# First batch of a fused attention and feed-forward kernel: another order of its prologue, without bank marking

## The chip, the cores and the metric

The kernel runs on one core of a Trainium2 chip. The metric is the device time of one execution in microseconds (us); lower is better. The kernel before takes 943.23 us (median of 3 runs, 943.13 to 943.5). A difference of more than 2% would count as faster or slower. Every profile lists the mean clock that was granted to TensorE; where it matters it is given.

## The reference

Eight batches of eight heads: queries of 576 tokens attend to keys and values that are first averaged over 8 tokens (72 pooled tokens). The result, 4608 rows of 512, goes through a hidden layer of 2048 with a periodic activation and an output layer.

```python
k_p = k.reshape(B, H, Sp, 8, D).mean(axis=3)          # v_p likewise
scores = scale * np.matmul(q, k_p.transpose(0, 1, 3, 2))
attn = softmax(scores)                                # sum + 1e-9
x = np.matmul(attn, v_p)                              # -> [4608, 512]
h = x @ w_in
g = h + sin(alpha * h) ** 2 / (alpha + 1e-9)
out = g @ w_out
```

All is in 32-bit floats. The kernel makes the two matrix products by Strassen's scheme (seven products of half size instead of eight), which is why sums of parts of w_in and of parts of x occur below.

## The kernel before

The time is that of a long, dense sequence of TensorE products. Ahead of it stands a prologue, `first_batch`: attention of batch 0, four score tiles of 128 rows (a fifth of 64 rows follows in the first products). One tile goes like this: TensorE makes scores, VectorE their maxima, ScalarE the exponentials, VectorE sums and reciprocals, GpSimd multiplies, TensorE transposes the probabilities, ScalarE and VectorE copy the transposes, TensorE multiplies with the values.

```python
def score_exp(i):
    sums = self.sm.tile([P, H], F32, name="sm")
    ps, odd = products(i)                               # scores, TensorE
    ...                                                 # max, shift: VectorE
    for hp in range(NP):                                # even heads; sums on the way
        nc.scalar.activation(out=E(n, i, h, h + 1), in_=ps[:n, hp:hp + 1, :], func=AF.Exp,
                             bias=mx[:n, hp:hp + 1], accum_out=sums[:n, h:h + 1])
    nc.scalar.activation(out=ex[:n, i, 1::2, 0:Sp], in_=..., func=AF.Exp)   # odd heads
    def rest(eng=nc.vector):
        ...                                             # sums of the odd heads, + 1e-9
        divide(i, sums, eng)
    return rest

def first_batch(self):
    ...                                                 # loads, transposed keys
    A.q_t(0)
    A.q_t(1)
    norm, v = {}, self.sum_v_rows(0)
    for i in range(4):
        norm[i] = A.score_exp(i)
        if i < 3:
            A.q_t(i + 2)
        if i:
            next(v)                                     # pooled values, TensorE
        if i:
            norm[i - 1](nc.gpsimd)
        if i > 1:
            self.mark(i - 2)
            A.a_t(i - 2, 0)                             # transposes of the probabilities
            A.a_t(i - 2, 1)
    ...                                                 # loads of the next keys, queries, w_in
    norm[3]()
    self.mark(2)
    A.a_t(2, 0)
    A.a_t(2, 1)
    self.mark(3)
    self.mark(4)
    A.a_t(3, 0)
    A.a_t(3, 1)
    for hp in range(4):
        A.values(hp)
    self.combine_w_in(0, 0)                             # sums of w_in, VectorE
    self.sums_of_x(0, 0)
    self.sums_of_x(0, 1)
```

The marking is four idle products with the identity, which write a PSUM bank whole. It is there because later a ScalarE copy fills a bank and TensorE accumulates onto the copy:

```python
def mark(self, i):
    ps = self.bank([P, 4, P], i)
    for j in range(4):
        self.nc.tensor.matmul(ps[:, j, :], self.ident[:], self.ident[:], start=(j == 0), ...)

def left0(G=G, Q=before):
    G.b6 = bank()
    nc.scalar.copy(out=G.b6[:], in_=G.b1[:])            # products 6 and 3 accumulate onto it
```

The hidden layer then runs in groups of seven products, in the order 1, 5, 6, 2, 7, 3, 4 (the numbers are those of the scheme, so product 7 is the fifth in time), and work of other kinds is hung into numbered slots, one for each product, before it:

```python
at(0, self.combine_w_in, 0, 1)
at(1, lambda: self.rest.append(A0.score_exp(4)))        # fifth tile
at(2, lambda: self.rest.pop()())
...
for J in range(1, 4):                                   # w_in parts 1 to 3
    at((4, 10, 14)[J - 1], self.combine_w_in, J, 0)
    at((6, 12, 20)[J - 1], self.combine_w_in, J, 1)
```

## Time and profile before

| | |
|---|---|
| time | 943.23 us (3 runs, 943.13 to 943.5) |
| span of the profiled run | 941.8 us |
| TensorE | 98% busy |
| first query transposes | 13.19 us |
| first values product | 33.95 us |
| product 7 of the first group | 46.84 us |

The busy line and the chain are shown in the prediction. This is the list of what TensorE waited for: the instruction that waited, what released it, then us in total, the number of times, and the longest.

```profile
PE ps_at L269 <- DVE aT L271: 1.2, 1, 1.2
PE bank L497 <- ACT bank L535: 0.8, 2, 0.6
PE bank L497 <- DVE as L373: 0.8, 1, 0.8
```

Apart from waits for the first loads these are all the waits of weight: 2.8 us. Idle time is thus no large prize; the other prize is TensorE work that computes nothing, the marks.

### The profile page before, as it was taken

How to read it: one execution, taken by the hardware profiler on the slowest of the kernel's cores; microseconds unless marked ns; L12 is line 12 of the kernel's file. 1: busy time of each engine (PE TensorE's matmuls, PEld its weight loads, DVE VectorE, ACT ScalarE, POOL GpSimd, SP SyncE). 2: the span in 40 equal slices, each digit the busy share in tenths (PEclk: the TensorE clock that was granted, in tenths of full speed). 3: DMA queues.
4: the chain of work that ended last, by engine and by line, in shares of the span. 5: the costliest groups of instructions: out<-in, count | busy, mean ns of one | idle time of the engine just before them, and what ended most of it. 6: DMA issues, size and time to landing. Idle time of an engine off the chain costs nothing.

```text
span 941.8 us, 17546 instructions
## 1 busy us (share of the span) xinstructions
PE 920.8 (98%) x6859; PEld 819.5 (87%) x6859; DVE 694.5 (74%) x1043; ACT 445.6 (47%) x1042; POOL 197.9 (21%) x214
## 2 busy tenths in 40 slices
PE   5999999999999999999999999999999999999997
PEld 3687787887878878787888899999999999999997
DVE  5779584766748677484346889988989798889794
ACT  5477576585857758677696651212111111211111
POOL 1628354453634536250000000000000000000000
PEclk9999999999999999999999999999999999999999
DMA  9645457666576663745624545353435444343501
GB/s 230 178 142 173 122 190 167 201 160 201 154 195 194 167 191 101 186 148 146 224 90 143 187 141 150 103 164 89 148 105 135 118 127 127 117 135 93 160 13 38
DMA packets 139777, 137.82 MB, mean 146 GB/s; under 512 B 49024, under 2 KB 108176, under 8 KB 139696
## 3 DMA queue, kind: packets, MB, share of 16 engines
q1 hardware_dynamic: 138624, 135.53, 49.8%
q10 hardware_dynamic: 1072, 1.19, 0.5%
q8 instruction: 54, 0.88, 0.4%
q14 instruction: 27, 0.22, 0.1%
HBM read 74.46 MB, written 47.19 MB: 129 GB/s over the span
## 4 chain that ended last, share of the span: by engine, by line
PE 94%; DVE 2%; ACT 2%; DMA 1%; issue 0%; SPq 0%; ACTq 0%; DVEq 0%
PE bank L497 45%; PE bank L778 29%; PE ps_y L778 12%; PE ps_o L311 3%; PE ps_sc L210 2%; DMA q<-in_q_dram 1%; DVE as L373 1%; PE ps_qt L191 1%; PE ps_at L269 1%; ACT s L503 1%; PE bank L460 1%; DVE home L470 0%; PE ps_or L320 0%; PE bank L122 0%; DVE a L373 0%
## 5 line engine op out<-in xcount | busy, mean ns | idle before, releaser
L497 PE MATMUL bank<-home,a 128*128 128x256 f32 x1152 | 267.1, 383 | 0.8 <-ACT bank L535 0.8
L497 PEld LDWEIGHTS bank<-home,a 128*128 128x128 f32 x1152 | 214.8, 190 | 35.8 <-ACT bank L535 2.7
L497 PE MATMUL bank<-home,as 128*128 128x256 f32 x864 | 202.4, 383 | 1.2 <-DVE as L373 0.8
L497 PEld LDWEIGHTS bank<-home,as 128*128 128x128 f32 x864 | 161.2, 190 | 26.4 <-ACT bank L523 3.2
L107 POOL TENSOR_TENSOR kvin<-kvin 72x512 f32<-72x512 f32 x112 | 122.2, 1091 | 164.2 <-DMA kvin<-in_v_dram 108.8
L778 PE MATMUL bank<-s,wb 128*128 128x144 f32 x896 | 119.4, 286 | 0.4 <-ACT bank L891 0.4
L778 PEld LDWEIGHTS bank<-s,wb 128*128 128x128 f32 x896 | 113.7, 190 | 0.7 <-ACT bank L891 0.6
L510 ACT ACTIVATE s<-s,c 128x256 f32<-128x256 f32 (+1 forms) x216 | 110.0, 573 | 0.0
L503 ACT ACTIVATE s<-h,al 128x256 f32<-128x256 f32 x144 | 65.2, 501 | 79.6 <-DVE h L476 79.6
L476 DVE TENSOR_TENSOR h<-bank,p 128x512 f32<-128x512 f32 x72 | 49.2, 683 | 62.8 <-ACT s L510 28.2
L891 ACT COPY bank<-bank 128x144 f32<-128x144 f32 x56 | 14.7, 263 | 145.7 <-PE bank L778 144.3
L503 ACT ACTIVATE s<-bank,al 128x256 f32<-128x256 f32 x144 | 59.9, 467 | 33.5 <-PE bank L497 10.5
L564 DVE TENSOR_TENSOR h<-bank,s 128x512 f32<-128x512 f32 x36 | 24.6, 684 | 49.7 <-ACT s L510 49.0
L910 ACT COPY bank<-bank 128x144 f32<-128x144 f32 x56 | 14.7, 263 | 88.2 <-PE bank L778 88.2
L252 POOL TENSOR_TENSOR ex<-ex,sm 128x576 f32<-128x576 f32 (+1 forms) x38 | 42.7, 1148 | 60.0 <-DVE sm L251 29.1
L733 DVE TENSOR_TENSOR s<-r 128x576 f32<-128x576 f32 x64 | 48.1, 752 | 0.8
L564 DVE TENSOR_TENSOR h<-h,s 128x1024 f32<-128x1024 f32 x36 | 46.2, 1283 | 0.0
L733 DVE TENSOR_TENSOR s<-x 128x576 f32<-128x576 f32 x48 | 36.2, 753 | 7.6 <-PE ps_y L778 6.7
L868 ACT COPY bank<-ps_y 128x288 f32<-128x288 f32 x56 | 21.4, 383 | 38.7 <-PE ps_y L778 38.7
L147 DVE STREAM_TRANSPOSE tr<-q 128x1024 f32<-128x1024 f32 (+1 forms) x24 | 18.1, 808 | 26.8 <-DMA g_bridge<-h 21.3
L778 PE MATMUL bank<-s,a 128*128 128x144 f32 x256 | 36.6, 286 | 0.0
L778 PE MATMUL ps_y<-s,a 128*128 128x144 f32 x256 | 36.6, 286 | 0.0
(142 smaller groups left out, 1436.4 us busy)
## 6 DMA issues: line engine op xcount, KB each, us to landing
g_bridge<-h SPq DMA_DIRECT2D x72, 512.0 KB
r<-g_bridge SPq DMA_DIRECT2D x31, 1152.0 KB
out_dram<-o SPq DMA_DIRECT2D x128, 72.0 KB
q<-in_q_dram SPq DMA_DIRECT2D x8, 1024.0 KB
kvin<-in_k_dram SPq DMA_DIRECT2D x28, 288.0 KB
kvin<-in_v_dram SPq DMA_DIRECT2D x28, 288.0 KB
a<-in_moe_w_in_dram SPq DMA_DIRECT2D x16, 256.0 KB
q<-tr SPq DMA_DIRECT2D x48, 80.0 KB
```

The source lines that it names most:

```text
L107: (eng or nc.gpsimd).tensor_tensor(out=o, in0=t[:, :, 0:w], in1=t[:, :, w:2 * w], op=OP.add)
L210: nc.tensor.matmul(ps[e][r:r + q.shape[-1], hp, :], q[s], kb[s, hp, :], start=True, stop=True)
L252: eng.tensor_tensor(out=E(n, i, 0, H), in0=E(n, i, 0, H), in1=sm[:n].unsqueeze(2).to_broadcast([n, H, Sp]), op=OP.mult)
L311: nc.tensor.matmul(ps[64 * e:64 * e + 64, :], vp[:, h, :], x, start=True, stop=True)
L476: add = lambda o, x, y: nc.vector.tensor_tensor(out=o, in0=x, in1=y, op=OP.add)
L497: nc.tensor.matmul(ps[:, jj, :], self.A[p][:, kk, f * P:(f + 1) * P], x[:, kk, :], start=(start and jj == 0 and kk == 0), stop=(kk == 1), ...
L503: nc.scalar.activation(out=G.s[:, i, jj, j, :], in_=src[:, jj], func=AF.Sin, scale=self.al[:, f:f + 1])
L510: nc.scalar.activation(out=x, in_=x, func=AF.Square, scale=self.c[:, f:f + 1])
L564: add = lambda o, x, y: self.nc.vector.tensor_tensor(out=o, in0=x, in1=y, op=OP.add)
L733: tt = lambda o, x, y, op: nc.vector.tensor_tensor(out=o, in0=x, in1=y, op=op)
L778: nc.tensor.matmul(out, W[:, J // 2, J % 2, :], A[:, J, :], start=(start and J == 0), stop=(J == self.NJ - 1), skip_group_check=True)
L868: nc.scalar.copy(out=x0[:], in_=yz[:, 0:1, :].to_broadcast([P, 2, T]))
```

## The change

It wants TensorE to reach the hidden layer earlier. The scores are issued one tile ahead, so that no engine waits for the next one's turn; the softmax sums come out of one reduction over all heads; the marks go, because the first two values products now write the two banks that need it (2 and 4) whole; the sums of w_in's first part are made while TensorE multiplies with the values. Also the fifth tile's division moves from VectorE to GpSimd and three w_in sums from slot 20 to slot 15.

```diff
-        def score_exp(i):
+        def soft(i, ps):
-            sums = self.sm.tile([P, H], F32, name="sm")
-            ps, odd = products(i)
+            even, odd = ps
 ...
-                nc.scalar.activation(out=E(n, i, h, h + 1), in_=ps[:n, hp:hp + 1, :], func=AF.Exp,
-                                     bias=mx[:n, hp:hp + 1], accum_out=sums[:n, h:h + 1])
+                nc.scalar.activation(out=E(n, i, h, h + 1), in_=even[:n, hp:hp + 1, :], func=AF.Exp, bias=mx[:n, hp:hp + 1])
 ...                                     (rest() goes; norm(i) was there already)
         def values(hp):
-            ps = self.ps_a.tile([P, 4 * P], F32, name="ps_o", tag="a")
+            ps = self.bank([P, 4 * P], 2 + 2 * hp) if b == 0 and hp < 2 else self.ps_a.tile([P, 4 * P], F32, name="ps_o", tag="a")
 ...                                     (mark() goes)
-        norm, v = {}, self.sum_v_rows(0)
+        v = self.sum_v_rows(0)
+        ps = A.products(0)
+        A.q_t(2)
         for i in range(4):
-            norm[i] = A.score_exp(i)
+            A.soft(i, ps)
             if i < 3:
-                A.q_t(i + 2)
-            if i:
+                ps = A.products(i + 1)
+                if i < 2:
+                    A.q_t(i + 3)
                 next(v)
             if i:
-                norm[i - 1](nc.gpsimd)
-            if i > 1:
-                self.mark(i - 2)
-                A.a_t(i - 2, 0)
-                A.a_t(i - 2, 1)
+                A.norm(i - 1)
+        A.a_t(0, 0)
+        A.a_t(0, 1)
+        A.norm(3)
+        A.a_t(1, 0)
+        A.a_t(1, 1)
 ...                                     (loads as before)
-        norm[3]()
-        self.mark(2)
-        A.a_t(2, 0)
-        A.a_t(2, 1)
-        self.mark(3)
-        self.mark(4)
-        A.a_t(3, 0)
-        A.a_t(3, 1)
+        for i in (2, 3):
+            A.a_t(i, 0)
+            A.a_t(i, 1)
+        self.combine_w_in(0, 0)
+        self.combine_w_in(0, 1)
         for hp in range(4):
             A.values(hp)
-        self.combine_w_in(0, 0)
 ...
-            at(0, self.combine_w_in, 0, 1)
-            at(1, lambda: self.rest.append(A0.score_exp(4)))
-            at(2, lambda: self.rest.pop()())
+            at(1, lambda: A0.soft(4, A0.products(4)))
+            at(2, A0.norm, 4)
 ...
-                at((6, 12, 20)[J - 1], self.combine_w_in, J, 1)
+                at((6, 12, 15)[J - 1], self.combine_w_in, J, 1)
```

More of the change, by code (lines that the diff above doesn't have):

```diff
@@ L227, in exp @@
             nc.scalar.activation(out=e, in_=e, func=AF.Exp, scale=scale)
-        def score_exp(i):
+        def soft(i, ps):
             n = rows[i]
-            sums = self.sm.tile([P, H], F32, name="sm")
-            ps, odd = products(i)
+            even, odd = ps
             mx = self.sm.tile([P, NP], F32, name="mx")
-            nc.vector.tensor_reduce(out=mx[:n], in_=ps[:n], axis=AX, op=OP.max, negate=True)
+            nc.vector.tensor_reduce(out=mx[:n], in_=even[:n], axis=AX, op=OP.max, negate=True)
             shift(i, 1, odd)
@@ L238, in score_exp @@
                 h = 2 * hp
-                nc.scalar.activation(out=E(n, i, h, h + 1), in_=ps[:n, hp:hp + 1, :], func=AF.Exp,
-                                     bias=mx[:n, hp:hp + 1], accum_out=sums[:n, h:h + 1])
+                nc.scalar.activation(out=E(n, i, h, h + 1), in_=even[:n, hp:hp + 1, :], func=AF.Exp, bias=mx[:n, hp:hp + 1])
             nc.scalar.activation(out=ex[:n, i, 1::2, 0:Sp], in_=ex[:n, i, 1::2, 0:Sp], func=AF.Exp)
-            def rest(eng=nc.vector):
-                nc.vector.tensor_reduce(out=sums[:n, 1::2], in_=ex[:n, i, 1::2, 0:Sp], axis=AX, op=OP.add)
-                nc.vector.tensor_scalar(out=sums[:n], in0=sums[:n], scalar1=1e-9, scalar2=None, op0=OP.add)
-                divide(i, sums, eng)
-            return rest
         def divide(i, sm, eng):
@@ L321, in values_rest @@
             to_x(ps[:], slice(0, NP), 512, 64)
-        return SimpleNamespace(**{f.__name__: f for f in (k_t, q_t, score, exp, score_exp, norm, new_a, a_t, turn, move, values, values_rest)})
+        return SimpleNamespace(**{f.__name__: f for f in (k_t, q_t, products, soft, score, exp, norm, new_a, a_t, turn, move, values, values_rest)})
     def load_alpha(self, rows):
@@ L454, in bank @@
         return self.ps_m.tile(shape, F32, name=f"bank{i}")
-    def mark(self, i):
-        ps = self.bank([P, 4, P], i)
-        for j in range(4):
-            self.nc.tensor.matmul(ps[:, j, :], self.ident[:], self.ident[:], start=(j == 0), stop=(j == 3), skip_group_check=True)
     def sums_of_x(self, u, n):
@@ L948, in run @@
                 self.qm, self.qt, self.kp, self.vp = {}, {}, {}, {}
-                self.bt, self.left, self.group, self.rest, self.turn = {}, [], None, [], 0
+                self.bt, self.left, self.group, self.turn = {}, [], None, 0
                 self.R = {}
```

## The prediction

> **What bounds the kernel now.** I read the page's busy table first, then the chain that ended last, then that chain in order of time over the first 100 us, then the timeline of each engine there.
>
> ```profile
> PE 920.8 (98%) x6859; PEld 819.5 (87%) x6859; DVE 694.5 (74%) x1043; ACT 445.6 (47%) x1042; POOL 197.9 (21%) x214
> PE 94%; DVE 2%; ACT 2%; DMA 1%; issue 0%; SPq 0%; ACTq 0%; DVEq 0%
> ```
>
> TensorE is busy for 98% of the span and carries 94% of the chain, so what counts is how early it gets through the prologue. After 100 us the waits of its matmuls add up to 0.4 us (one, in the output phase). So whatever the first 100 us gain reaches the end unchanged, and nothing later can add to it. The change touches only these first 100 us. The chain there (start, us, what):
>
> ```profile
> 23.76 1.09 PE bank L460 x8
> 24.85 0.87 PE ps_at L269 x8
> ...
> 27.33 1.09 PE bank L460 x8
> 28.42 0.87 PE ps_at L269 x8
> 29.29 0.89 PE bank L460 x8
> 30.19 0.87 PE ps_at L269 x8
> 31.06 1.79 PE bank L460 x16
> 32.85 0.45 PE ps_at L269 x4
> ...
> 33.95 3.68 PE ps_o L311 x16
> ...
> 38.28 0.86 DVE home L470 x2
> ...
> 44.67 1.30 ACT ex L239 x8
> ...
> 46.30 0.49 ACT bank L535
> ...
> 46.84 1.99 PE bank L497 x8
> ```
>
> L460 is the bank marking: five marks of four 128x128 products, 1.09 + 1.09 + 0.89 + 1.79 = 4.86 us, all on the chain. Up to 33.3 us TensorE runs without a break; L269 are the transposes of the probabilities, L311 the values products. From 38.3 to 46.8 us the chain leaves TensorE: VectorE makes the sums of x (L470) and of w_in (L373), then the maximum of the fifth score tile (L235), ScalarE its exponentials (L239, L241) and the bank copy L535 for which the product at 46.84 waits. In that stretch TensorE sits idle 0.79 us (until 42.89, for L373) and 0.3 us (until 46.84). Later idle times: 0.21 us until 76.34, 0.59 us until 80.65 (both ACT copies) and 1.20 us until 90.92, where a transpose waits for VectorE's copy L271, which stood behind three w_in sums.
>
> VectorE in that stretch (start, us, instruction):
>
> ```profile
> 34.37 0.68 DVE L373 TENSOR_TENSOR as<-a,a 128x512 f32<-128x512 f32 x1
> ...
> 39.86 1.75 DVE L470 TENSOR_TENSOR home<-home,home 128x512 f32<-128x512 f32 x1
> 41.54 1.21 DVE L373 TENSOR_TENSOR as<-as,a 128x512 f32<-128x512 f32 x1
> 42.67 0.94 DVE L373 TENSOR_TENSOR a<-a,a 128x512 f32<-128x512 f32 x1
> ```
>
> The same operation takes 0.68 us alone and 0.94, 1.21 or 1.75 us while GpSimd makes its key sums (29.8 to 43.05 us).
>
> **What the Trainium skill says.** "PSUM — Partial Sum Buffer", section "The four PSUM rules": only TensorE sets the bits that make a later product accumulate; a ScalarE copy into a bank leaves them as they are. Here banks filled by a ScalarE copy (L523, L535) are accumulated onto, so they must first have been written whole by TensorE. Only the first two such banks (numbers 2 and 4) see no whole product before; values products of 128x512 into exactly those do a mark's work for nothing. The trace shows no such bits. "SBUF — State Buffer", section "Who interferes with whom": a VectorE operation with two SBUF inputs and a GpSimd operation reading SBUF lock each other out; the four durations above agree, and reductions do not contend (0.44 to 0.46 us throughout). "ScalarE: Activation LUTs", section "What ACT_TABLE_LOAD costs": a load takes about 1283 ns (trace: 1.28 us at 15.80), and activations in a row overlap by about 93 ns. "TensorE: Matmul & The Clock Gate", section "Part 1: The HAM clock gate": after an idle window of about 3.4 us the array falls to half clock. The trace shows a warm-up: the 64x72 products take 0.38 us at 15.19 and 0.22 us from 18.04 on.
>
> **The change, part by part.** I replay the new order of each engine (taken from the built program) with the durations of this trace.
>
> *Scores ahead, one table load later.* Products 0 to 3, the query transposes and the value sums keep their durations; with neither mark 0 nor the first transposes in between, products 3 start at 23.7 instead of 25.72 us and the last value sum (L125, 0.95) ends at 25.3 instead of 27.3 us. ScalarE now copies the third query tile before the exponentials: the copy waits for the transposes (17.45), and the table load follows it, 18.0 to 19.25 instead of 15.80 to 17.08. The first exponentials are 2.2 us later, but TensorE's next need, the copy of query tile 3, is met by 21.06, well before 23.7.
>
> *Sums in one operation.* The exponentials lose their accumulator reads (four a tile; starts 0.30 us apart become, as an estimate from duration minus the page's overlap, 0.22): about 0.3 us per tile off ScalarE. VectorE replaces a reduction of 0.44, an addition of 0.17 and its wait by one reduction over eight heads of 0.76 (row L259): about 0.1 us more per tile. Neither binds.
>
> *Marks gone, but a wait in their place.* After 25.3 us the chain is that of the last tile. ScalarE: copy of the value sums at 25.3, exponentials of tile 3 from 25.8 to 27.1 (ends with L241's form). VectorE: sum and reciprocal 27.2 to 28.2. GpSimd multiplies 28.3 to 29.45 (1.15). TensorE transposes tile 3 at 29.5 to 30.4 (0.87), ScalarE copies 29.97 to 30.55, and the values products start at 30.6 instead of 33.95. TensorE idles about 1.0 us (a transpose waits for a buffer that ScalarE frees at 27.6) plus 0.5 us and 0.2 us. Check: 4.86 removed less some 1.5 of new idle time is 3.35 us, the difference 33.95 - 30.6.
>
> *w_in sums during values.* Values end at 34.3 instead of 37.6. VectorE starts its eight two-input sums at 31.0 instead of in two pieces until 44.2. Besides GpSimd, starts are 0.86, 1.13 or 1.68 us apart, so eight take about 8.9 us and end at 39.9. The first sum of x is ready at 36.2, the second at 37.9, the third at 39.05. TensorE: product 1 34.3 to 36.2, fifth scores to 36.85, then three products of 1.77 each, to 42.2, without a wait. The fifth tile's maximum is at 39.9, its exponentials 40.4 to 41.6, the bank copy to 42.15: just in time for the product at 42.2 instead of 46.84. That gains 9.2 - 7.9 = 1.25 us more. Sum: 3.35 + 1.25 = **4.6 us**.
>
> *Fifth tile's division on GpSimd.* It queues behind the key sums, ends at some 43.6 to 44.0; its transposes are due at 44.0. No loss, barely.
>
> *Three w_in sums moved earlier (slot 20 to 15).* They leave the place where they cost 1.20 us (90.92) and stand before four softmax sums and the addition h (L476, in before at 83.51) which the seventh group's last product must await, as it writes the same bank. I find that addition ending 1.2 us after the product could start. So the 1.2 us change place: net 0, give or take 0.7.
>
> **Rivals.**
> 1. *A transfer holds the lead back.* In the issue queue's waits, w_in's second part lands at 42.9 to 45.1 us and queries 1 at 41.4 to 42.3. They are issued behind the fourth key load, which waits for GpSimd's first key sum; that moves only some 0.4 us. TensorE wants the queries at 44.6 and the weights at 50.7, VectorE its first of them at 43.9: against this rival, by 1 us. If it held, it would take back up to 2 us: 940.5.
> 2. *VectorE becomes the bound.* Its eight sums beside GpSimd end just in time. If each costs 0.3 us more, the fifth softmax comes 2 us later and the gain falls to 2.5: 940.7. For it: durations up to 1.75 us. Against it: GpSimd is through at 42.2 anyway.
> 3. *The array's clock falls.* Between 26.2 and 30.5 us TensorE works only some 2.7 of 4.4 us. If that lowered the clock, values and the first products would take longer by 2 to 4 us: 940.5 to 943. No gap is longer than 1.1 us, so I give it one in twelve.
> 4. *Both stalls of the moved sums vanish,* if GpSimd's value sums end earlier: 1.2 us more gain, 937.4.
>
> **Range and chances.** 943.23 - 4.6 = 938.6. Rivals 1 to 3 pull up to 941.2, the fourth and a shorter softmax chain down to 937.0. Over 2% would need 18.9 us; all marks and all the idle times listed above make 4.86 + 3.1 = 8 us, so faster is next to excluded; slower would need a lasting clock loss.
>
> **What would show it.** Right: no L460 rows; values products from about 30.6; product seven of the first group near 42.2; the idle time at 90.9 gone and one of about 1.2 us some 5 us earlier for an addition of h; busy time of TensorE down by some 4.5 us. Wrong: values later than 32 us, matmuls of 128x256 slower than 0.38 us after the gap, or TensorE waiting for a DMA between 42 and 60 us.

## The result, and the profile after

The changed kernel takes 940.89 us (median of 4 runs, 939.70 to 941.32); the kernel before took 943.37 us on the same chip (4 runs, 943.13 to 944.28). The ratio is 0.997, 95% interval 0.9953 to 0.9987. That is the same within 2%, as predicted, and inside the predicted range, but the gain is 2.5 us by the medians and not 4.6. A ratio here and below is the mean time of one kernel's fast runs over that of the other's fast runs in the same rounds, so it is not quite the ratio of the medians quoted.

The busy line and the chain's shares of the changed kernel:

```profile
PE 916.1 (98%) x6819; PEld 814.8 (87%) x6819; DVE 691.3 (74%) x1036; ACT 444.3 (47%) x1022; POOL 200.1 (21%) x216
PE 93%; DVE 3%; DMA 2%; ACT 1%; issue 1%; SPq 1%; POOL 0%; DVEq 0%; ACTq 0%; POOLq 0%
```

TensorE works 4.7 us less, as the marks are gone. But VectorE has a larger share of the chain than before, and a transfer has come onto it. The chain's pieces in order of time (start, us, what):

```profile
27.36 1.16 POOL ex L244
...
29.87 1.94 PE bank L304 x8
...
36.90 8.23 DMA a<-in_moe_w_in_dram
...
45.22 0.06 DVE as L366
...
46.51 0.34 DVE aT L263
...
46.98 0.63 PE ps_qt L191 x4
```

L304 is the values product: it starts at 29.87 us and not at 33.95. From 36.9 us the chain runs through a load of the second part of w_in, VectorE's first sum of it (L366), and a copy (L263) that stands behind that sum in VectorE's queue, to a query transpose. That is a new path. What TensorE waited for now (columns as before):

```profile
PE bank L484 <- DVE h L463: 1.5, 1, 1.5
PE ps_at L261 <- ACT aT L263: 0.9, 1, 0.9
PE bank L484 <- ACT bank L522: 0.8, 2, 0.6
PE ps_qt L191 <- DVE aT L263: 0.4, 1, 0.4
...
PE ps_at L261 <- DVE aT L263: 0.3, 1, 0.3
PE ps_at L261 <- POOL ex L244: 0.3, 1, 0.3
```

The wait of 1.2 us for a copy of transposes has shrunk to 0.3; the wait for w_in sums is gone; 0.9 and 0.4 us are new, and so is 1.5 us for the addition of h. The two that matter most on TensorE's timeline (start, us, operation, count, in brackets the idle time before and what ended it):

```profile
41.66 1.99 PE L484 MATMUL bank<-home,a 128*128 128x256 f32 x8 [0.19 <-ACT bank L522]
81.07 1.99 PE L484 MATMUL bank<-home,a 128*128 128x256 f32 x8 [1.50 <-DVE h L463]
```

The first is product 7 of the first group, 46.84 us in the kernel before; the second is the last product (product 4) of the third group. VectorE's timeline in the same kernel:

```profile
30.28 0.68 DVE L366 TENSOR_TENSOR as<-a,a 128x512 f32<-128x512 f32 x1
...
32.88 1.75 DVE L366 TENSOR_TENSOR as<-a,as 128x512 f32<-128x512 f32 x1
...
45.22 0.69 DVE L366 TENSOR_TENSOR as<-a,a 128x512 f32<-128x512 f32 x1 [3.00 <-DMA a<-in_moe_w_in_dram]
```

The w_in sums begin at 30.28, beside the values products, and the fifth tile follows them early enough. At 45.22 VectorE has stood still for 3.00 us for the load.

Two profiles do not start alike: the queries land at a different moment in each. So stretches are compared, from the first query transpose ("query start") on. The last column is the sum: from there to the second product (product 5) of the fourth group, behind which the two kernels do the same.

| profile | query start | to first values product | to product 7 of group 1 | to product 1 of group 2 | to product 5 of group 4 | sum |
|---|---|---|---|---|---|---|
| before | 13.19 | 20.76 | 12.89 | 8.43 | 36.62 | 78.70 |
| before, second profile | 13.37 | 20.50 | 12.88 | 8.44 | 36.45 | 78.27 |
| changed | 12.55 | 17.32 | 11.79 | 8.97 | 37.15 | 75.23 |
| changed, second profile | 12.99 | 17.81 | 11.80 | 8.92 | 36.89 | 75.42 |

Means: 20.63 to 17.57 (gain 3.1), 12.89 to 11.80 (gain 1.1), 8.44 to 8.95 (loss 0.5), 36.5 to 37.0 (loss 0.5): 3.2 us in all.

### The profile page after: what moved, and what is told of

Same layout as the page of the kernel before. It is cut to its first block, busy times and chain, and to the rows that moved or that the text cites. A ratio compares the mean times of both kernels' runs of the same rounds, so it can differ in the third digit from the quotient of the medians.

```text
span 937.9 us, 17446 instructions
## 1 busy us (share of the span) xinstructions
PE 916.1 (98%) x6819; PEld 814.8 (87%) x6819; DVE 691.3 (74%) x1036; ACT 444.3 (47%) x1022; POOL 200.1 (21%) x216
## 4 chain that ended last, share of the span: by engine, by line
PE 93%; DVE 3%; DMA 2%; ACT 1%; issue 1%; SPq 1%; POOL 0%; DVEq 0%; ACTq 0%; POOLq 0%
PE bank L484 44%; PE bank L764 29%; PE ps_y L764 12%; PE ps_o L304 3%; PE ps_sc L210 2%; DMA q<-in_q_dram 1%; DMA a<-in_moe_w_in_dram 1%; PE ps_qt L191 1%; PE ps_at L261 0%; DVE sm L251 0%; DVE h L463 0%; PE ps_or L313 0%; PE bank L122 0%; DVE as L366 0%; DVE a L366 0%
## 5 line engine op out<-in xcount | busy, mean ns | idle before, releaser
L244 POOL TENSOR_TENSOR ex<-ex,sm 128x576 f32<-128x576 f32 (+1 forms) x40 | 45.0, 1149 | 55.5 <-DVE sm L243 30.7
L764 PE MATMUL ps_y<-r,wb 128*128 128x144 f32 x256 | 36.6, 286 | 0.0
L764 PE MATMUL bank<-r,wb 128*128 128x144 f32 x256 | 36.6, 286 | 0.0
```

Of the source, the lines that this page charges most:

```text
L244: eng.tensor_tensor(out=E(n, i, 0, H), in0=E(n, i, 0, H), in1=sm[:n].unsqueeze(2).to_broadcast([n, H, Sp]), op=OP.mult)
L764: nc.tensor.matmul(out, W[:, J // 2, J % 2, :], A[:, J, :], start=(start and J == 0), stop=(J == self.NJ - 1), skip_group_check=True)
```

## The experiments

All outputs are right. Edits are given against the changed kernel unless something else is said.

**Controls.** The unedited changed kernel once more, and at the end the unedited kernel before for a second profile.

> The changed kernel unedited, beside the others. Theory A (the prologue gains 3.4 us at the values products and 4.5 us at the seventh product, as predicted, and some is given back later to w_in's second part landing at about 45 us and to the moved sums): 940.9 us, give or take 0.6; in the profile the values products stand 17.8 us after the first query copy starts (29.87 - 12.07; before: 33.95 - 12.71 = 21.24), and VectorE idles 2 to 3.5 us until its first w_in sum of the second group, near 45. Theory B (the gap between 3.9 us in the profiles and 2.5 us in the medians is only the moment at which the first queries land): the distance from the query copy to product one of the second group is the same 38.6 us in every profile, and only the copy's start (12.0 to 13 us) moves.

939.77 us (5 runs, 939.63 to 941.16) against 943.80 (11 runs, 942.73 to 945.09); ratio 0.996, interval 0.9947 to 0.9972. With the first result this puts the gain at 2.8 to 3.8 us, and the sum of stretches gives 3.2. Theory A had the wait for the load right (2.96 us) but its time, 940.9 give or take 0.6, lay above the 939.77 measured. Theory B's fixed distance of 38.6 us failed: it is 39.0 here (51.52 less 12.51).

> The kernel before, unedited, for a second profile of it: if the array's warm-up moment is as random there as in the changed kernel, its first fast 64x72 product comes 4 to 8.3 us after the first query transpose, and the stretch from there to the first values product lies between 20.5 and 21.5 us; product seven of the first group stands 12.8 to 13.0 us after the first values product, as in its first profile (12.89). A value of 11.8 there would show that the later w_in sums cost it nothing in some runs.

One run of 943.52 us, of unknown state. Product seven stands 12.88 us after the first values product and the stretch to values is 20.50: the profile of before was no accident.

**Marks alone: the kernel before without its marks,** its first two values products in banks 2 and 4. Edit against the kernel before:

```diff
-            ps = self.ps_a.tile([P, 4 * P], F32, name="ps_o", tag="a")
+            ps = self.bank([P, 4 * P], 2 + 2 * hp) if b == 0 and hp < 2 else self.ps_a.tile([P, 4 * P], F32, name="ps_o", tag="a")
 ...
-                self.mark(i - 2)
-        self.mark(2)
-        self.mark(3)
-        self.mark(4)
```

> The kernel before with one part of the change alone: no bank marking, and the first two values products write banks 2 and 4. Worked out from the trace of before: the values products start at 31.3 instead of 33.95 us and everything behind follows, so 2.6 us off before, as much as the whole change brings in the medians. Rival (the marks filled time in which TensorE would have waited for the last tile's softmax anyway): under 1 us off before.

945.93 us (6 runs, 942.47 to 946.43), ratio 1.0016, interval 1.0004 to 1.0029: slower than the kernel before. The expectation missed. Five runs had a granted clock of 0.991 or 0.992 and took 945.67 to 946.43; the sixth had 0.998 and took 942.47. TensorE's timeline of the profiled run, which was one of the five:

```profile
29.01 1.07 PE L269 MATMUL ps_at<-ident,ex 128*72 128x128 f32 x8 [1.56 <-POOL ex L252]
30.94 1.65 PE L269 MATMUL ps_at<-ident,ex 128*72 128x128 f32 x8 [0.86 <-DVE ex L252]
32.52 3.68 PE L311 MATMUL bank<-aT,vp 72*64 72x512 f32 x8
...
39.54 3.78 PE L497 MATMUL bank<-home,a 128*128 128x256 f32 x8
```

The eight values products take 3.68 us (1.94 in the changed kernel), the eight products of the hidden layer 3.78 (1.99). The same run by stretches; the second column is the length, then busy us and instructions of TensorE, its weight loads, VectorE, ScalarE and GpSimd, then the granted clock and the transfers:

```profile
28.00:32.00 4.00, 2.13 (x15) 1.78 (x16) 3.29 (x6) 1.50 (x4) 3.84 (x5) 0.90 0.00 0
32.00:44.00 12.00, 12.00 (x39) 5.11 (x39) 5.73 (x9) 3.31 (x6) 8.00 (x9) 0.50 0.97 283
```

TensorE was busy for only 2.13 of 4.00 us, and the clock went to 0.50. By the packed trace's own record (trace.npz) it stayed there from 31.22 to 44.87 us, although TensorE then worked without a break. In the changed kernel TensorE is busy for 3.44 us of the same four, and the granted clock is 1.00 throughout. So in the old order the marks did something besides marking: they filled the gaps. To test that reading, two marks went back into the gaps, one ahead of the transposes of tile 2 and one ahead of those of tile 3 (against the kernel just told):

```diff
+        self.mark(0)
         A.a_t(2, 0)
         A.a_t(2, 1)
+        self.mark(1)
         A.a_t(3, 0)
```

> The kernel of e4_marks_only (before without marks), with two marks of four products put back, not where TensorE has work, but into its two waits for the softmax (1.56 us before the third tile's transposes, 0.86 us before the fourth's). Clock theory: in e4 the clock fell to half from 31 to 44.6 us because TensorE idled; filled with work that nobody needs, the waits keep it at full speed, the mean clock is 0.998 to 0.999 in all runs, and the kernel is 1.3 to 2 us faster than before (e4's one run without the fall was 1.3 us faster). Rival (the clock fell for another reason, or by chance): runs of about 946 us at a clock of 0.991 or 0.992 as in e4.

942.19 us (5 runs, 940.96 to 943.19), before 944.18 there (9 runs, 942.65 to 945.72), ratio 0.9979, interval 0.9965 to 0.9994; clock 0.998 to 1.0 in all five runs. More idle products and a shorter time, with the clock kept in all five runs: the fall of the clock was what had made the marks-only kernel slow. TensorE's longest wait in that stretch is now 0.67 us. Removing the marks from the old order is thus worth 1.3 us (the one run at 0.998) to 2 us (with two marks kept) if the clock holds, and costs some 2 if it does not.

**The marks in the new order.** The changed kernel with all five marks back ahead of the transposes:

```diff
+        self.mark(0)
         A.a_t(0, 0)
 ...
+        self.mark(1)
         A.a_t(1, 0)
 ...
         for i in (2, 3):
+            self.mark(i)
+            if i == 3:
+                self.mark(4)
             A.a_t(i, 0)
```

> The changed kernel with the five marks put back in front of the transposes, everything else as changed. Theory: the marks fill part of about 1.5 us in which TensorE waits for the last tile's softmax, so 4.46 us of marks (five of 0.89) cost 3 to 3.5 us, and the kernel stands 0.5 to 1.5 us below before. Rival (the reordering is the gain, the marks are nearly free beside the waits): within 1.5 us of the changed kernel.

942.73 us (5 runs, 942.11 to 944.06), ratio 0.9986, interval 0.9973 to 0.9998. Values start 20.11 us after query start, against 17.32 and 17.81: the marks cost 2.3 to 2.8 us there, some 2.4 us by the ratios (0.9986 less 0.996 of 943 us), less than the 3 to 3.5 expected. The new order and the earlier w_in sums alone give some 1.3 us.

**The w_in sums in their old place.**

```diff
-        self.combine_w_in(0, 0)
-        self.combine_w_in(0, 1)
         for hp in range(4):
             A.values(hp)
+        self.combine_w_in(0, 0)
 ...
+            at(0, self.combine_w_in, 0, 1)
```

> The changed kernel with the first group's w_in sums where they stood before: one behind the values products, three in the first slot of the hidden stage. Prediction's step: 1.25 us of gain come from these sums during the values, so the product seven of the first group starts about 12.9 us after the values products instead of 11.8, and the kernel is 1.1 us slower than the changed one. Rival (what is gained there is lost again to w_in's second part, which lands at 44 to 46 us whatever is before it): less than 0.5 us slower.

942.33 us (5 runs, 942.24 to 944.19), ratio 0.9983, interval 0.997 to 0.9996. The stretch from values to product seven is 13.55 us instead of 11.80, and TensorE's timeline has the old wait back:

```profile
41.68 1.97 PE L484 MATMUL bank<-home,as 128*128 128x256 f32 x8 [0.79 <-DVE as L366]
```

This part alone is worth 1.75 us by the profile, more than the 1.25 predicted. The earlier the values come, the more a late sum seems to cost: with the sums in their old place the stretch is 12.89 us where values start 20.76 us after query start (before), 13.26 at 19.34 (two marks in the gaps) and 13.55 at 18.26 (here).

**The transfer.** The second part of w_in loaded right behind the first, so that nothing can wait for it:

```diff
         self.load_w_in_part(0)
+        self.load_w_in_part(1)
 ...
         self.load_q(1)
-        self.load_w_in_part(1)
```

> The second part of w_in is asked for right after the first, before the keys of batch 1, in the time from 24 to 33 us in which no transfer runs. Theory A: the 3.0 us for which VectorE stands idle until 45.22 shrink below 0.7 us, the 0.44 us wait of a query transpose at 46.98 goes, and the kernel is 0.4 to 1.5 us faster than the control, with less spread between its runs. Rival (the wait is hidden: TensorE had work until then): within 0.3 us of the control.

940.12 us (5 runs, 939.57 to 941.15), ratio 0.9962, interval 0.995 to 0.9974: no difference from the control on the same chip (0.996), so the gain of 0.4 to 1.5 us that theory A expected did not come. VectorE's sum starts without a wait at 43.26:

```profile
43.26 0.71 DVE L366 TENSOR_TENSOR as<-a,a 128x512 f32<-128x512 f32 x1
```

The 0.4 us of TensorE's wait went, and a wait of 0.26 us for GpSimd's division of the fifth tile (at 45.03) came in its place; the stretch shrank from 8.92 to 8.67. Other profiles show that the load's landing is a matter of chance: in the next experiment, which does not touch it, VectorE waited for it only 0.56 us instead of 3.00 and 2.96, and the stretch was 8.36, no longer than in the kernel before:

```profile
44.10 1.27 DVE L366 TENSOR_TENSOR as<-a,a 128x512 f32<-128x512 f32 x1 [0.56 <-DMA a<-in_moe_w_in_dram]
```

So the transfer takes 0.5 us in some executions and nothing in others. That lies within the scatter of the times.

**The three moved sums back in slot 20.**

```diff
-                at((6, 12, 15)[J - 1], self.combine_w_in, J, 1)
+                at((6, 12, 20)[J - 1], self.combine_w_in, J, 1)
```

> The three w_in sums of the last group back from slot 15 to slot 20. Prediction's step: net 0, give or take 0.7 us, against the control: the 1.50 us wait of the product behind the addition h at 81.07 goes, and a wait of about 1.2 us of a transpose behind VectorE's copy returns near 86. Rival: the move costs more than it brings, and this run is faster than the control by 0.8 us or more. Other rival: the move is the gain it was meant to be, and this run is slower by 1.2 us.

940.44 us (5 runs, 940.13 to 940.85), ratio 0.9963, interval 0.9951 to 0.9975: neutral. The wait of 1.20 us at a transpose is back (at 87.09) and the one of 1.5 us is gone, as the swap in the prediction has it.

**The fourth tile's division first.** `A.norm(3)` ahead of `A.a_t(0, 0)` instead of behind it, so that VectorE's copies do not stand before the chain of the last tile:

> The changed kernel with the last tile's sum and reciprocal put in front of the first copies of transposes on VectorE. If the chain of the last tile (sum, reciprocal, GpSimd's division, transposes, copy) sets the start of the values products, as predicted, they start 0.5 us earlier: 17.3 us instead of 17.8 us after the first query transposes of the profile, and the kernel is 0.3 to 0.6 us faster. Rival (the transposes' wait of 0.88 us for ScalarE's copies sets it): no difference.

940.57 us (5 runs, 940.24 to 941.11), ratio 0.9961, interval 0.9949 to 0.9974: nothing to see in the time, and the half us expected did not come. Its profile has 17.97 us to the first values product, against 18.33 in the profile of the preceding experiment; but that difference is not the edit's.

That last remark needs explaining. In every profile but that of the last experiment below, the 64x72 products of the scores are slow at first (0.32 to 0.38 us) and fast later (0.22 us). The moment at which the array becomes fast is kept in the packed trace: its record of the granted clock has its first entry there, and the clock columns print 1.00 for the time before it. In the changed kernel that is at 16.23 us (four query transposes take 0.89 us at 15.72 and 0.66 us at 17.28). Counted from query start it came after 3.57 to 6.18 us in the twelve profiles without idle products ahead of the queries. In the new order without marks the stretch to values follows it: 17.32 us at a delay of 3.68, 17.55 at 4.21, 17.64 at 4.65, 17.81 at 5.01, 18.26 at 6.02, 18.33 at 6.18. The run with the division first, 17.97 at 5.34, lies on the same line, so the edit did nothing there.

**The w_in sums a group earlier still.** The sums of w_in's parts 2 and 3 (J in the code, which counts from 0) ahead of the softmax sums of the second batch:

```diff
-                at((4, 10, 14)[J - 1], self.combine_w_in, J, 0)
-                at((6, 12, 15)[J - 1], self.combine_w_in, J, 1)
+                at((4, 7, 10)[J - 1], self.combine_w_in, J, 0)
+                at((6, 8, 12)[J - 1], self.combine_w_in, J, 1)
```

> The changed kernel with the six w_in sums of its three later parts issued a products group earlier than needed: slots 7 and 8 for the second part instead of 10 and 12, slots 10 and 12 for the third instead of 14 and 15. In the changed kernel the last product of the seventh group waits 1.50 us at 81.07 for VectorE's addition of h, which stands behind the third part's sums; in three other profiles the same wait is 1.10 us. If the moved sums are what took the rest of the gain, that wait goes, no wait takes its place, and the time is 1.0 to 1.5 us under the changed kernel run twice before (939.8 to 940.9): 938.3 to 939.8. Rival: the sums, some 4 us of VectorE each part, now delay the score tiles of the second batch that VectorE makes in those slots, and the wait only changes its place: time within 0.5 us of the changed kernel, with a new TensorE wait of 0.5 to 1.5 us somewhere between 55 and 80 us.

938.34 us (5 runs, 938.10 to 938.67), before 943.39 there (9 runs, 942.64 to 944.49), ratio 0.9944, interval 0.9932 to 0.9957. All five runs lie below all nine timed runs of the unedited changed kernel (939.63 to 941.32). VectorE, then TensorE in this kernel's timeline:

```profile
79.13 0.68 DVE L463 TENSOR_TENSOR h<-bank,p 128x512 f32<-128x512 f32 x1
```

```profile
79.87 1.99 PE L484 MATMUL bank<-home,a 128*128 128x256 f32 x8
```

The addition of h is through before the product wants its bank, and the product has no wait. No wait of TensorE has come up elsewhere, and the last stretch is 35.73 us instead of 37.15 and 36.89. The place of these sums was worth 1.2 to 1.4 us, and neither slot 20 nor slot 15 was the right one.

**Idle products ahead of the queries,** to make the array fast before it is needed: four with the identity behind the first small transpose, two behind each of the first three key transposes, four behind the fourth, in a bank that is free then.

```diff
+    def warm(self, n):
+        ps = self.bank([P, 4, P], 3)
+        for j in range(n):
+            self.nc.tensor.matmul(ps[:, j, :], self.ident[:], self.ident[:], start=(j == 0), ...)
 ...
         self.turn_alpha()
+        self.warm(4)
 ...
                 nc.tensor.transpose(ps[:, hp, :], kp[...], ...)      # k_t
+                if b == 0:
+                    self.warm(2 if hp < 3 else 4)
```

> The changed kernel with fourteen idle 128x128 products of the identity before the first query transposes, in a bank that is free then (four after the first small transpose, two after each of the first three key transposes, four after the fourth). Theory: the scatter of the runs (1.5 us) and the missing part of the gain come from the moment at which the array's products become fast, which came 4.05 to 8.3 us after the first query transpose in the profiles so far. If idle products bring that moment to or before the first query transpose, the stretch from there to the first values product shrinks from 17.3 to 18.3 us to 16.3 to 16.7, the time is 0.8 to 1.8 us under the changed kernel (938.0 to 940.0) and its runs lie closer together than 1 us. Rival: that stretch is bound by the copies and exps of ScalarE and GpSimd and not by products, so that it stays at 17.3 or more and the time stays within 0.5 us; or the idle products hold back the query transposes and the time grows by their 1 to 2 us.

939.34 us (5 runs, 938.20 to 939.89), ratio 0.9953, interval 0.994 to 0.9965. The median lies in the range of the theory, but the theory is not borne out by this run: the runs scatter over 1.7 us as before, and in the profile the array was still slow when the queries came. The first fast product came 4.37 us after query start, and values 17.54 us after it.

**All three together** (sums earlier, division first, idle products):

> The changed kernel with three edits together: the w_in sums a group earlier, the idle products ahead of the queries, and the division of the fourth tile ahead of the first copies of the transposed keys. If the gains of the first two add up, 2 to 3 us under the changed kernel, 937.0 to 938.5, and a ratio to the kernel before of 0.993 to 0.995. If neither does anything, 939.5 to 941, a ratio of 0.996 to 0.997. If only one of them does, in between, and the two runs beside it say which.

937.58 us (5 runs, 936.65 to 938.27), ratio 0.9936, interval 0.9923 to 0.995. It is the fastest kernel and beats both the kernel before, by some 6 us, and the changed one, by some 2 to 3. Here the idle products did their work in the profiled run. TensorE's timeline, the last idle products and the first query transposes of this run:

```profile
10.72 2.01 PE L455 MATMUL bank<-ident 128*128 128x128 f32 x8
13.20 1.10 PE L193 MATMUL ps_qt<-ident,q 128*128 128x128 f32 x8 [0.47 <-DVE q L93]
```

and the first query transposes of the changed kernel:

```profile
12.55 1.97 PE L191 MATMUL ps_qt<-ident,q 128*128 128x128 f32 x8 [2.21 <-DVE q L93]
```

The same eight transposes take 1.10 us and not 1.97, and the values start 16.58 us after query start. So an array that is fast at once is worth about 1 us there; but the same fourteen idle products got it there in one profile and not in the other. Over the sums alone (0.9944) the three together give 0.8 us, which the intervals do not resolve.

One more build was not run: the new order without any whole write of the banks by TensorE, neither marks nor values. A product accumulates in bank 4 where no product of the kernel has set or cleared the bits for it before. What such a bank would give on the chip stays open.

## Why the prediction was right or wrong

**Class and range: right.** 940.89 us lies inside 937.0 to 941.2, and faster or slower by 2% was excluded by the same sum. The point, 938.6, is 2.3 us too low for that batch and 1.2 for the control. The failed steps are terms of the sum of 4.6 us.

**"3.35" for values earlier: right.** 30.6 less the query start of that profile (13.19) is 17.41; measured 17.32 and 17.81. The idle time was put at about 1.0, 0.5 and 0.2 us and measured 0.89, 0.33 and 0.23 (the last was there before too). What this step did not say: nearly all of the stretch's gain, 20.63 to 17.57, is the marks. With the marks back it is 20.11, but there the array became fast 3.57 us after query start, and 4.81 and 4.22 us after it in the two profiles of before. At 0.4 us of stretch for each us of that delay, the slope of the six pairs above, an estimate leaves 0.1 to 0.2 us for the order and 2.8 for the marks. That is less than the 3.6 that 4.86 less 0.89 and 0.33 us would give, because the idle times understate the waits: from the first transpose of probabilities, or the mark ahead of it, to the values the changed kernel takes 5.62 us and the run with the marks back 8.46, of which 4.57 are marks, counted from start to start. So the waits cost 1.73 us and not 1.22, and 4.57 less 1.73 is 2.84.

**"1.25" for w_in sums during values: right in mechanism, a little short in size.** The stretch to product seven shrank by 1.1; undone alone it costs 1.75. One line is misread: the sum of 0.68 us at 34.37 was not "alone", as GpSimd worked from 32.76 to 35.63 us; the one at 43.53, behind GpSimd's last sum, was. The estimate of 8.9 us for the eight sums does not hang on it (9.1 in the changed kernel, 30.28 to 39.36).

**Rival 1, the transfer, rejected "by 1 us": here the prediction failed, by a small term.** The landing, said to lie between 42.9 and 45.1, was right (the load ends at 45.13 on the chain). Wrong was when VectorE would want it: 43.9 in the prediction, but VectorE was idle from 42.2 on. Nor did the prediction see how it would reach TensorE: not through the weights, wanted at 50.7, but through a copy that stands behind the sum in VectorE's order. It costs 0.5 us in both profiles of the unedited changed kernel, nothing in some others, and loading earlier did not move the time.

**"No loss, barely" for the fifth tile's division on GpSimd: right.** TensorE waits for it only in the run with the earlier load, 0.26 us.

**"Net 0, give or take 0.7" for the three moved sums: right, on the bad side.** The wait of 1.20 us fell to 0.34; in its place came 1.50, or 1.10 in other profiles. (The prediction calls that group the seventh by a slip; it is the third, J = 2 in the code.) With all that lies between, the stretch is 0.5 us longer. With the sums back in slot 20 the time is the same. The prediction asked which of two places is better, and the experiment shows that a third gives 1.2 to 1.4 us.

**Rival 3, the clock, "one in twelve": right for this kernel, but the reason given was not enough.** The lowest clock of any run of the changed kernel is 0.998. But removing the marks from the old order lost the clock in five runs of six, and there too TensorE's gaps were short, 1.56 us at most; what differs is how much it was busy (see the last section). The prediction took the marks for pure cost; in the old order they also bridged gaps. The new order made them unnecessary for that, which is why the parts of this change do not add up one by one.

**Rival 2, VectorE, did not occur:** the wait ahead of product seven is 0.19 us. **Rival 4 did not occur** with slot 15. Its size, 1.2 us, is what the earlier sums brought, by another way than the one that the rival named.

**Left out of the prediction: the scatter.** Runs of the changed kernel differ by up to 1.7 us, those of the kernel before by up to 3.1. Two sources are seen in the profiles, the moment at which the first queries are there (query start 12.55 to 14.48) and the moment at which the array becomes fast, which moves the values by up to 1.0 us (17.32 to 18.33); how the scatter divides between them is open.

Sum: the first gain fell short by 0.3 us, the second by 0.15, the transfer took 0.5, the moved sums 0.5. That is about 1.4 of the 4.6, which leaves 3.2, the stretches' sum.

## What to carry to other kernels

Before removing idle TensorE products ask what else they do: between short pieces of work they may keep the clock up, and then their removal pays only together with an order that closes the gaps. An engine that runs ahead still delays others through its own queue: place work that has slack ahead of the work that the bound engine awaits, and try more than two places. When parts interlock, test each alone and each missing: here one part alone made the kernel slower, and the same part was the largest gain within the whole.

## What the Trainium skill lacked or had wrong

- "TensorE: Matmul & The Clock Gate", section "Part 1: The HAM clock gate": the page has the array fall to half clock after an idle window of about 3.4 us and come back after a busy one of that length. The length agrees: in the fourteen packed traces the granted clock changes, after its first entry, only at whole multiples of 3.413 us (4, 263, 269 or 270 of them: 13.65, 897.71, 918.19 and 921.60 us). But the window need not be idle. Cut into stretches of that length from the first entry on, the full-clock time of these traces shows a fall at the end of every stretch with TensorE busy for 1.34 us or less (1.34 in the marks-only run, where no wait was longer than 1.56 us; 1.22, 1.16 and about 0 at the ends of kernels), and no fall after one with 1.45 us or more (1.45 at the end of a kernel, 1.91 in the midst of one). The page gives no such share; it only tells of a kernel whose short idle times made the clock swing. Nor did one busy window bring the clock back: in the marks-only run it took four, in all of which TensorE was busy throughout. Where these stretches lie may be why one run of six kept its clock; that is not shown, as only one of the six has a profile.
- The same section gives about 4 us, give or take 0.5, until sustained products become fast. Counted from the first query transposes it was 3.57 to 6.18 us in the twelve profiles without idle products. In all fourteen the array became fast at the end of the first such stretch of 3.41 us in which TensorE was busy for 3.13 us or more: with idle products a stretch of 3.13 us did it at 12.92 us in the run of all three, and stretches of 3.07, 2.83 and 2.89 us did not in the run of the idle products alone, where it came at 17.95.
- No page says how to read a profile ahead of the first entry of the clock's record. The clock columns take that time as full: they read 1.00 from 4 to 18 us in the run where products were slow until 17.95.
